# Sixteen loads issued by ScalarE instead of SyncE in a cluster-attention and softplus-FFN kernel

## The chip, the cores and the metric

The kernel runs on one core of a Trainium2 chip. Time is device time in microseconds (us) for one execution of the whole program. Its engines work from queues of their own, in order: TensorE (PE, with the weight loads PEld beside it), VectorE (DVE), ScalarE (ACT), GpSimd (POOL) and SyncE (SP), which computes nothing and issues DMAs.

## The reference, cut to what matters

Attention over 4 batches, 8 heads, 768 positions of 64 numbers, in which a query sees only the keys of its own cluster (16 centroids for each head); then a dense feed-forward with a softplus.

```
q_assign = argmax(einsum(q / |q|, c / |c|));  k_assign = the same of k
scores   = where(q_assign == k_assign, q k^T / 8, -1e9)
attn     = softmax(scores) @ v                       # (4, 8, 768, 64)
x        = attn as 3072 tokens of 512
out      = softplus(x @ w_in) @ w_out                # w_in 512 x 2048, w_out 2048 x 512
```

The weights come as 64-bit floating point, the rest as 32-bit.

## The kernel before, in words

Products are made in 16-bit halves (a high part and what it leaves over), so most data are cast to a high part and subtracted to a low part before a matmul uses them.

**Passes and tiles.** Eight passes `pi`: four batches, two halves of 384 queries each. A tile `t` is one head `n` and 128 queries; there are 24 tiles to a pass, 192 in all. Tiles 0 to 23 (pass 0) take the way of `upright`, where scores come out already turned. From tile 24 on, `scores(t)` is a chain of six steps: PE multiplies queries by keys into `s` (L1079), DVE takes the row maximum `negm` (L1095), ACT the exponential `p` (L1103), ACT or POOL the high part (`ph<t>`, L1112), POOL or DVE the low part (`p<t>`, L1113), and SP issues a transposing DMA `pt<-phl` (`flip`, L307, called in L1133). `attend(t)` then multiplies `pt` by the values into `mbank` (L1173 to L1175). Four pairs of heads make an `x`, which is transposed too (`xT`), and `ffn1` (L1244 to L1246, 16 blocks of 128 columns a pass), `softplus` (L1265, L1266, L1281) and `ffn2` (L1645 to L1647) follow, one pass behind attention.

**Preparation.** `prep_k`, `prep_q` and `prep_v` load keys, queries and values of two or four heads (384 KB each; 192 KB for the first halves), cast and subtract them, transpose them (from head 4 on by DMA: `kt<-kn`, `qt<-qn`, `qt<-n`) and find the clusters. `prep_weights(step)` loads one of 32 blocks of weights (512 KB, steps 0 to 15 of `w_in`, 16 to 31 of `w_out`) as raw 64-bit words into room that is later used by other data, and turns it into two 16-bit halves: ACT (L414), then `wb` (L372 or L374), DVE (L421), `wh` (L424), `w` (L425 to L429). The loads wait for room: a block for the block that had the same room before, keys, queries and values of later heads for one of two `raw` buffers.

**What sets the order.** Every piece of work is an operation of a generator. `either(key, first, second)` has two engines for it, and the key's presence in `SWAPPED` takes the second. The string `PLAN` names, two characters an operation, which generator goes next; there are 3543 of them, and since each engine runs its own instructions in order, `PLAN` is the order of every queue. The numbers in ns beside the operations (450 for a load) served when the string was made; nothing reads them when the kernel is built. `FILL` puts idle matmuls (L266) ahead of some of the first PE operations. Before the change all loads, stores and transposes are issued by SP, so they wait for each other in that one queue.

Of the kernel before, what the change touches and what calls it, by code (L numbers as in the profile page):

```python
# [37 lines left out]
SWAPPED = ('E1_0', 'S1l_1', 'S1l_3', 'S2_1', 'S2_3', 'S2h_0', 'S2l_0', 'S3l_0', 'S3l_2', 'S4_0', 'S4_2', 'S4_3', 'S4h_2', 'S4l_1', 'S4l_2', 'T1a_0', 'T1a_1', 'T1a_2', 'T1a_3', 'T1c_1', 'T1c_2', 'T1c_3', 'T1h_1', 'T1h_3', 'T1l_3', 'T2a_0', 'T2a_2', 'T2c_0', 'T2c_2', 'T2h_1', 'T2h_2', 'T2h_3', 'T2l_0', 'T2l_2', 'T2l_3', 'T3a_0', 'T3a_1', 'T3a_2', 'T3a_3', 'T3b_0', 'T3b_2', 'T3c_0', 'T3c_1', 'T3h_0', 'T3h_2', 'T3h_3', 'T3l_1', 'T3l_2', 'T3l_3', 'T4a_0', 'T4h_2', 'T4h_3', 'T4l_0', 'T4l_2', 'g0_2', 'g0_3', 'g0_6', 'g0_7', 'g1_1', 'g1_3', 'g2_0', 'g2_2', 'g3_1', 'g3_3', 'g3_4', 'g3_5', 'g3_7', 'g4_2', 'g4_4', 'g4_6', 'g5_5', 'g5_7', 'g6_1', 'g6_5', 'g7_1', 'g7_2', 'g7_4', 'g7_5', 'g7_6', 'g7_7', 'gh1_0', 'gh1_1', 'gh1_4', 'gh1_5', 'gh1_6', 'gh2_2', 'gh2_3', 'gh2_4', 'gh2_5', 'gh3_1', 'gh3_2', 'gh3_3', 'gh3_4', 'gh3_5', 'gh3_6', 'gh3_7', 'gh4_0', 'gh4_1', 'gh4_2', 'gh4_3', 'gh4_4', 'gh4_5', 'gh4_7', 'gh5_0', 'gh5_1', 'gh5_2', 'gh5_3', 'gh5_4', 'gh5_6', 'gh6_0', 'gh6_2', 'gh6_3', 'gh6_6', 'gh7_0', 'gh7_2', 'gh7_3', 'gh7_5', 'k0_0', 'k10', 'k16', 'k2', 'kT0_0_1', 'kT0_2_1', 'kT1_0_1', 'kT1_2_0', 'kT1_2_1', 'kh18', 'kh2', 'kh22', 'kh24', 'kh28', 'kh30', 'kh6', 'm12_2_0', 'm16_4_0', 'm4_0_0', 'mw_0', 'p103', 'p104', 'p108', 'p109', 'p111', 'p113', 'p115', 'p126', 'p138', 'p141', 'p142', 'p154', 'p157', 'p162', 'p165', 'p168', 'p174', 'p176', 'p182', 'p183', 'p187', 'p190', 'p191', 'p25', 'p27', 'p29', 'p30', 'p31', 'p33', 'p34', 'p35', 'p36', 'p37', 'p39', 'p40', 'p43', 'p44', 'p45', 'p58', 'p61', 'p63', 'p69', 'p76', 'p84', 'p85', 'p86', 'p87', 'p89', 'p95', 'p96', 'p98', 'ph100', 'ph102', 'ph103', 'ph104', 'ph106', 'ph107', 'ph108', 'ph109', 'ph110', 'ph111', 'ph112', 'ph115', 'ph116', 'ph117', 'ph119', 'ph120', 'ph121', 'ph122', 'ph123', 'ph124', 'ph125', 'ph126', 'ph127', 'ph128', 'ph129', 'ph130', 'ph131', 'ph133', 'ph135', 'ph136', 'ph137', 'ph140', 'ph141', 'ph142', 'ph143', 'ph145', 'ph146', 'ph147', 'ph149', 'ph150', 'ph151', 'ph152', 'ph153', 'ph154', 'ph156', 'ph157', 'ph158', 'ph159', 'ph160', 'ph163', 'ph164', 'ph165', 'ph167', 'ph168', 'ph169', 'ph170', 'ph171', 'ph173', 'ph174', 'ph175', 'ph176', 'ph177', 'ph178', 'ph181', 'ph184', 'ph185', 'ph189', 'ph190', 'ph24', 'ph28', 'ph36', 'ph42', 'ph48', 'ph50', 'ph51', 'ph52', 'ph53', 'ph56', 'ph59', 'ph60', 'ph63', 'ph65', 'ph66', 'ph68', 'ph71', 'ph75', 'ph76', 'ph78', 'ph80', 'ph81', 'ph82', 'ph83', 'ph86', 'ph87', 'ph88', 'ph89', 'ph90', 'ph91', 'ph94', 'ph95', 'ph97', 'ph98', 'ph99', 'q0_0_0', 'qT0_0', 'qT1_1', 'qh4_0', 'u1', 'u10', 'u2', 'u21', 'u22', 'u23', 'u27', 'u31', 'u33', 'u35', 'u9', 'v10', 'v2', 'v22', 'v28', 'v30', 'v8', 'vh0', 'vh12', 'vh14', 'vh16', 'vh18', 'vh20', 'vh22', 'vh24', 'vh26', 'vh28', 'vh30', 'vh8', 'w10', 'w11', 'w16', 'w18', 'w20', 'w21', 'w26', 'w31', 'w9', 'wb0', 'wb1', 'wb10', 'wb12', 'wb13', 'wb14', 'wb15', 'wb16', 'wb17', 'wb18', 'wb2', 'wb20', 'wb21', 'wb22', 'wb23', 'wb24', 'wb25', 'wb26', 'wb27', 'wb28', 'wb30', 'wb31', 'wb4', 'wb5', 'wb7', 'wb8', 'wb9', 'wh1', 'wh12', 'wh13', 'wh14', 'wh15', 'wh16', 'wh17', 'wh21', 'wh23', 'wh24', 'wh26', 'wh27', 'wh29', 'wh3', 'wh30', 'wh31', 'wh5', 'wh6', 'wh7', 'wh8', 'x1_3', 'x2_2', 'x3_0', 'x4_2', 'x5_2', 'x6_1', 'x7_1', 'x7_3', 'xh0_0', 'xh0_2', 'xh0_3', 'xh1_0', 'xh1_1', 'xh1_3', 'xh2_0', 'xh2_1', 'xh2_2', 'xh3_0', 'xh4_1', 'xh4_2', 'xh5_1', 'xh5_2', 'xh6_0', 'xh6_1', 'xh6_2', 'xh6_3', 'xh7_0', 'xh7_2', 'xh7_3', 'zk0', 'zk10', 'zk14', 'zk16', 'zk22', 'zk26', 'zk28', 'zk30', 'zk4', 'zk8', 'zq0_0_1', 'zq0_1', 'zq12_2', 'zq12_3', 'zq16_4', 'zq24_6', 'zq24_7', 'zq28_6', 'zq28_7', 'zq4_1', 'zq8_2', 'zq8_3')  # L38

REBASE = 2.0**-112  # L40
# [8 lines left out]
    "dodq081x1zdrcdcedrc821dy1u230acac7211z0723dw1wcb21210dcf2523dv1ycd2527c80d2327dpdr29ca0b20cd23290dcf2523dr1q"
    "2b2bcb2522cg22dz2d2bcg0cdx29250a1q2722e00d2d252d22272fcf2429cc2f2bc90dca0d0d2d27c9e2cgcbch26ce0dcf2h270d2h0d"  # L50
    "2928cdcicfchcg29e32b2jch0d0c2jci2b0d2a2fe4cg0dch2l0d2f2dci2h222dcj2cccck0dcje52n2lch2f2ncj2e2p2e2h222f2j2h0d"
    "0a2jck2e2pe72l2n2p0d2j2h2e1q2ncl2l2gcicc2l0c2p2i2j2nck22cj0d2lcecl2p0ecj2nci2eckcm2ece2pck2r2t0e2r2k0e2r2t2v"
    "2me80ccl2r2vcn2t2r2t2x2t2e2vcme92x2o2q2v2xclcm2v2z2q312xco2q0f2qcn2z310eeb0ecm2r2z31cocn2x0e2t312qec2s2vcl2u"
# [1670 lines left out]
```

## Time and profile before

| | |
|---|---|
| median of 3 runs | 804.58 us (803.59 to 806.15) |
| the profiled execution's own time | 803.36 us |
| its span, first to last instruction | 801.6 us |
| granted clock of TensorE | 1.00 throughout |
| PE busy | 782.3 us, 98% |
| PEld, DVE busy | 520.8 us (65%), 623.3 us (78%) |
| ACT, POOL busy | 450.4 us (56%), 632.1 us (79%) |
| DMA | 138.45 MB, 173 GB/s; 377 issues of SP in the plan, 259 of them transposes |

Busy time of an engine does not count the issuing of DMAs; an issue stands in the timeline of SP's queue (SPq), from its start until the queue goes on. "Idle before" is the time for which an engine stood still ahead of an instruction, and the arrow names what ended it. The chain of waits is followed back from the last instruction: at each step to what released it.

### The profile page before, as it was taken

How to read it: one execution, taken by the hardware profiler on the slowest of the kernel's cores; microseconds unless marked ns; L12 is line 12 of the kernel's file. 1: busy time of each engine (PE TensorE's matmuls, PEld its weight loads, DVE VectorE, ACT ScalarE, POOL GpSimd, SP SyncE). 2: the span in 40 equal slices, each digit the busy share in tenths (PEclk: the TensorE clock that was granted, in tenths of full speed). 3: DMA queues.
4: the chain of work that ended last, by engine and by line, in shares of the span. 5: the costliest groups of instructions: out<-in, count | busy, mean ns of one | idle time of the engine just before them, and what ended most of it. 6: DMA issues, size and time to landing. Idle time of an engine off the chain costs nothing.

```text
span 801.6 us, 19510 instructions
## 1 busy us (share of the span) xinstructions
PE 782.3 (98%) x7933; PEld 520.8 (65%) x7933; DVE 623.3 (78%) x977; ACT 450.4 (56%) x721; POOL 632.1 (79%) x521
## 2 busy tenths in 40 slices
PE   7999988999999999999999999999999999999998
PEld 6899655556566666556656666556656565676787
DVE  7998989878577869586787867676866768777796
ACT  6889979646656655355444455353554454625540
POOL 5787766758889879777589999888898898995463
DMA  8999999999999999999999999999998785730101
GB/s 271 257 239 240 204 235 234 244 224 178 195 195 197 188 189 169 225 193 196 154 156 210 187 187 184 181 176 210 170 157 172 127 160 90 141 61 1 47 2 60
DMA packets 411851, 138.45 MB, mean 173 GB/s; under 512 B 388464, under 2 KB 405360, under 8 KB 411760
## 3 DMA queue, kind: packets, MB, share of 16 engines
q1 hardware_dynamic: 411760, 137.19, 87.5%
q8 instruction: 62, 1.02, 0.5%
q14 instruction: 29, 0.24, 0.1%
HBM read 35.68 MB, written 6.29 MB: 52 GB/s over the span
## 4 chain that ended last, share of the span: by engine, by line
PE 79%; DMA 8%; ACT 4%; POOL 3%; DVE 2%; issue 1%; SPq 1%; POOLq 0%; DVEq 0%; ACTq 0%
PE s L1079 11%; PE h L1244 9%; PE h L1246 9%; PE h L1245 9%; PE o L1645 7%; PE o L1647 7%; PE o L1646 7%; PE mbank L1175 3%; PE mbank L1173 3%; PE mbank L1174 3%; DMA pt<-phl 3%; PE mbank L1169 3%; PE m L1523 2%; PE m L1522 2%; PE m L1524 2%
## 5 line engine op out<-in xcount | busy, mean ns | idle before, releaser
L1095 DVE TENSOR_REDUCE negm<-s 128x1 f32<-128x768 f32 x168 | 158.7, 951 | 79.3 <-PE s L1079 78.1
L1117 POOL TENSOR_TENSOR phl<-p,phl 128x768 f16<-128x768 f32 x117 | 204.3, 1752 | 7.2 <-ACT phl L285 4.3
L1103 ACT ACTIVATE p<-s,negm 128x768 f32<-128x768 f32 x168 | 150.0, 897 | 95.4 <-DVE negm L1095 72.5
L1244 PE MATMUL h<-xT,wi 128*128 128x384 f16 x512 | 166.7, 326 | 0.6 <-DVE fg L1281 0.6
L1246 PE MATMUL h<-xT,wi 128*128 128x384 f16 x512 | 166.9, 326 | 0.0
L1245 PE MATMUL h<-xT,wi 128*128 128x384 f16 x512 | 166.8, 326 | 0.0
L1265 ACT ACTIVATE fa<-h 128x384 f32<-128x384 f32 x128 | 62.5, 489 | 136.6 <-PE h L1246 136.4
L1079 PE MATMUL s<-kt,qt 128*128 128x384 f16 x672 | 134.4, 326 | 2.9 <-DMA qt<-n 1.8
L285 POOL CAST phl<-p 128x768 f16<-128x768 f32 x103 | 94.0, 917 | 46.9 <-ACT p L1103 23.9
L1173 PE MATMUL mbank<-vb,pt 128*128 128x65 f16 x1008 | 106.1, 192 | 6.2 <-DMA pt<-phl 6.1
L1647 PE MATMUL o<-wo,gh 128*128 128x512 f16 x288 | 109.1, 379 | 0.0
L1646 PE MATMUL o<-wo,gh 128*128 128x512 f16 x288 | 109.1, 379 | 0.0
L1645 PE MATMUL o<-wo,gh 128*128 128x512 f16 x288 | 109.1, 379 | 0.0
L1174 PE MATMUL mbank<-vb,pt 128*128 128x64 f16 x1008 | 106.1, 192 | 0.0
L1175 PE MATMUL mbank<-vb,pt 128*128 128x65 f16 x1008 | 105.7, 194 | 0.0
L1173 PEld LDWEIGHTS <-pt 128*128 128x128 f16 x1008 | 93.1, 98 | 18.8 <-DMA pt<-phl 9.1
L1174 PEld LDWEIGHTS <-pt 128*128 128x128 f16 x1008 | 92.8, 97 | 9.3
L1175 PEld LDWEIGHTS <-pt 128*128 128x128 f16 x1008 | 92.9, 97 | 0.0
L1079 PEld LDWEIGHTS <-qt 128*128 128x128 f16 x672 | 62.0, 98 | 44.4 <-DMA qt<-n 3.0
L1281 DVE SCALAR_TENSOR_TENSOR fg<-fa,h 128x384 f32<-128x384 f32 x104 | 56.2, 546 | 28.6 <-ACT fa L1266 24.2
L1246 PEld LDWEIGHTS <-wi 128*128 128x128 f16 x512 | 50.0, 98 | 33.2
L1244 PEld LDWEIGHTS <-wi 128*128 128x128 f16 x512 | 50.0, 98 | 31.8 <-issue 0.5
(309 smaller groups left out, 1645.0 us busy)
## 6 DMA issues: line engine op xcount, KB each, us to landing
wo<-in_moe_w_in_dram SPq DMA_DIRECT2D x16, 512.0 KB, 6.3
wo<-in_moe_w_out_dram SPq DMA_DIRECT2D x14, 512.0 KB, 4.8
rawk<-in_k_dram SPq DMA_DIRECT2D x15, 384.0 KB, 4.2
...
pt<-phl SPq DMA_TRANSPOSE x168, 4.2
...
```

The source lines that it names most:

```text
L1079: nc.tensor.matmul(st[:, j, :SH], qt[:, s, i], kt[:, s, NT // 2 * j : NT // 2 * (j + 1)], start=(s == 0), stop=(s == 1),)
L1095: yield op("DVE", 950, lambda: nc.vector.tensor_reduce(negm, st[:, :, :SH], AX.XY, ALU.max, negate=True))
L1117: lambda e: e.tensor_tensor(phl[:, u, 1], p32, phl[:, u, 0], ALU.subtract),
L1173: nc.tensor.matmul(av, pt[:, 0, c], vb[:, c, D : 2 * D + 1], start=(c == 0), stop=False)
L1174: nc.tensor.matmul(av[:, :D], pt[:, 0, c], vb[:, c, :D], start=False, stop=False)
L1175: nc.tensor.matmul(av, pt[:, 1, c], vb[:, c, D : 2 * D + 1], start=False, stop=(c == NT - 1))
L1244: nc.tensor.matmul(hp, w[0], x[0], start=(c == 0), stop=False)
L1245: nc.tensor.matmul(hp, w[0], x[1], start=False, stop=False)
L1246: nc.tensor.matmul(hp, w[1], x[0], start=False, stop=(c == NP - 1))
L1645: nc.tensor.matmul(po, g[0], wo[:, f, 0, 0], start=(f == f0), stop=False)
L1646: nc.tensor.matmul(po, g[0], wo[:, f, 0, 1], start=False, stop=False)
L1647: nc.tensor.matmul(po, g[1], wo[:, f, 0, 0], start=False, stop=(f == f0 + NF // 2 - 1))
```

## The change: what it does

Plain loads and stores get a key (`move`), so that ACT can be taken instead of SP. Sixteen keys are swapped; all else of that kind stays on SP, as do all transposes. `PLAN`, `SWAPPED` and `FILL` differ up to operation 1149 of 3543. From there on the order of every queue and the side of every operation are as before.

```diff
-FILL = {0: 26, 2: 3, 4: 8, 8: 3, 9: 3, 14: 19, 19: 9, 22: 4, 24: 4, 26: 3}
+FILL = {0: 26, 2: 3, 4: 11, 8: 4, 14: 15, 19: 8, 20: 3, 22: 4, 24: 3, 26: 3}
...
+    'lk1', 'lk12', 'lk14', 'lq12_2', 'lq8_3', 'lv10', 'lv12', 'lw13', 'lw22', 'lw23', 'lw25', 'lw26', 'lw29', 'lw30', 'lw5', 'lw6',
...
+ISSUE = 450
...
-    engines = {"DVE": nc.vector, "ACT": nc.scalar, "POOL": nc.gpsimd}
+    engines = {"DVE": nc.vector, "ACT": nc.scalar, "POOL": nc.gpsimd, "SP": nc.sync}
...
-    def load(dst, src, nbytes, ns=450):
-        return op("SP", ns, lambda: nc.sync.dma_start(dst, src), dma=nbytes / 290.0)
+    def move(key, dst, src, nbytes, ns=450, **opt):
+        return either(key, ("SP", ns), ("ACT", ISSUE), lambda e: e.dma_start(dst, src), dma=nbytes / 290.0, **opt)
...
-        yield load(raw64, src[:, c, e * WC : (e + 1) * WC], P * WC * 8)
+        yield move(f"lw{step}", raw64, src[:, c, e * WC : (e + 1) * WC], P * WC * 8)
...
-            yield load(kf, rows(k, n, 0, NT, 2), P * 2 * NT * D * 4)
+            yield move(f"lk{n}", kf, rows(k, n, 0, NT, 2), P * 2 * NT * D * 4)
```

The sixteen, with their place among the 3543 operations (read by following `PLAN` through `Order.run`) and the start of their issue by SP in the trace of before:

| load | place before, after | issued at, us |
|---|---|---|
| lk1 (head 1, second half of the first keys) | 6, 3 | 1.65 |
| lw5, lw6, lw13 | 175, 130; 200, 162; 329, 330 | 28.15; 28.84; 47.55 |
| lw22, lw23 | 569, 521; 592, 540 | 92.08; 96.45 |
| lw25, lw26 | 666, 669; 709, 691 | 114.42; 123.20 |
| lk12 | 807, 773 | 143.93 |
| lw29, lw30 | 852, 837; 880, 853 | 149.72; 152.63 |
| lk14, lv10 | 893, 883; 928, 887 | 156.27; 166.93 |
| lq12_2, lv12 | 947, 964; 989, 1001 | 169.28; 177.68 |
| lq8_3 | 1123, 1100 | 209.97 |

Other sides changed in the same stretch: 18 operations from DVE to POOL and 13 back, 23 from ACT to POOL and 19 back, 10 from DVE to ACT and 4 back. Of those between operations 500 and 870, ACT gives POOL the high parts `ph29`, `ph32`, `ph45`, `gh0_0`, `gh0_2`, `gh0_3`, `kh12`, and `wb21`, `wh25`, `wh28`; it takes from POOL `ph28`, `ph42`, `vh8`, `xh1_0`, `wb19`, `wb29`, `wh21`, `wh23`, `wh26`. `p25` goes from DVE to POOL, behind `p24`; `kh2`, at the start, from POOL to ACT, ahead of the second copy of the first turned keys.

In SP's queue some neighbours change places: the first queries' load stands third instead of fourth; the values of heads 8 and 9 (`lv8`) are loaded behind the transpose of tile 31 instead of ahead of it; tile 54 is transposed ahead of tile 55 instead of behind it.

## Rows read from the trace of the kernel before

**Rows 1.** Windows: busy us (instructions) of PE, PEld, DVE, ACT, POOL; clock; DMA share; GB/s

```profile
0.00:40.00 40.00, 34.64 (x496) 30.36 (x496) 34.28 (x105) 29.49 (x52) 25.99 (x40) 1.00 0.87 264
...
80.00:150.00 70.00, 63.94 (x670) 41.84 (x669) 63.12 (x100) 63.15 (x103) 49.47 (x38) 1.00 1.12 225
150.00:215.00 65.00, 61.66 (x594) 36.58 (x593) 48.24 (x84) 34.70 (x55) 49.27 (x41) 1.00 1.06 208
```

**Rows 2.** Waits of PE, 80 to 215 us: us in total, times, longest

```profile
PE mbank L1173 <- DMA pt<-phl: 5.5, 6, 1.7
```

**Rows 3.** Timeline of PE: start, us, instruction [idle before <-releaser]

```profile
88.86 0.20 PE L1173 MATMUL mbank<-vb,pt 128*128 128x65 f16 x1 [0.62 <-DMA pt<-phl]
...
115.07 0.20 PE L1173 MATMUL mbank<-vb,pt 128*128 128x65 f16 x1 [1.02 <-DMA pt<-phl]
...
139.31 0.20 PE L1173 MATMUL mbank<-vb,pt 128*128 128x65 f16 x1 [1.65 <-DMA pt<-phl]
...
159.41 0.42 PE L588 MATMUL sim_k<-cents,kt 128*128 128x32 f16 x10 [0.79 <-DMA kt<-kn]
...
179.84 0.34 PE L1079 MATMUL s<-kt,qt 128*128 128x384 f16 x1 [1.22 <-DMA qt<-n]
...
209.77 0.20 PE L1173 MATMUL mbank<-vb,pt 128*128 128x65 f16 x1 [1.33 <-DMA pt<-phl]
```

**Rows 4.** Chain of waits, parts of 0 to 215 us: start, us, what

```profile
2.13 4.37 DMA rawq<-in_q_dram
...
105.81 2.38 SPq L307
...
108.24 4.01 DMA rawv<-in_v_dram
...
143.93 3.55 DMA rawk<-in_k_dram
...
163.05 5.10 DMA wraw<-in_moe_w_out_dram
```

**Rows 5.** Timeline of SP's queue: start, us, issue

```profile
1.65 0.43 SPq L302 DMA_DIRECT2D rawk<-in_k_dram  x1
...
92.08 1.00 SPq L302 DMA_DIRECT2D wo<-in_moe_w_out_dram  x1
...
108.92 1.65 SPq L307 DMA_TRANSPOSE pt<-phl  x1
...
204.09 2.91 SPq L307 DMA_TRANSPOSE pt<-phl  x1
...
209.97 0.50 SPq L302 DMA_DIRECT2D rawq<-in_q_dram  x1
```

**Rows 6.** Transposes of tiles, 80 to 215 us: ns min/median/max, first and last start; landing

```profile
L307 SPq DMA_TRANSPOSE pt<-phl x34: 1273/1630/4162, 82.8 to 214.8; - x34
...
DMA to landing us min/median/max: 3.7/4.7/6.8
```

**Rows 7.** Timeline of DVE and POOL: the low parts of tiles 24, 25, 31, 54

```profile
80.78 1.97 POOL L1117 TENSOR_TENSOR phl<-p,phl 128x768 f16<-128x768 f32 x1
...
82.44 1.12 DVE L1117 TENSOR_TENSOR phl<-p,phl 128x768 f16<-128x768 f32 x1 [0.33 <-ACT phl L285]
...
102.91 1.25 DVE L1117 TENSOR_TENSOR phl<-p,phl 128x768 f16<-128x768 f32 x1
...
199.33 3.25 POOL L1117 TENSOR_TENSOR phl<-p,phl 128x768 f16<-128x768 f32 x2 [0.34 <-ACT phl L285]
```

**Rows 8.** Waits of ACT, 80 to 150 us

```profile
ACT wo L414 <- DMA wo<-in_moe_w_out_dram: 5.0, 3, 1.9
```

**Rows 9.** Lines of ACT, 80 to 150 us: busy us, mean ns | idle before

```profile
L285 ACT CAST phl<-p 128x768 f16<-128x768 f32 x17 | 14.0, 830 | 1.1 <-DMA pt<-phl 1.0
...
L372 ACT ACTIVATE wo<-wo 128x512 int32<-128x512 uint8 x10 | 6.7, 670 | 0.0
...
L285 ACT CAST wo<-wo 128x512 f16<-128x512 f32 x6 | 3.9, 648 | 0.0
```

More of the change, by code (lines that the diff above doesn't have):

```diff
@@ L49 @@
[L49 to L53, printed above, removed]
@@ new lines @@
+    "1hd4071f0bd908d409c6c71h1j1fd41h1f1j0b1h1ld4c81f1lc6dg091n1l1jc31j1f0b1h1g1n1hdic51p1jc5c7081p081n1j1rc4081i"
+    "c9090b1r1t1vc808c31p08dj081r1k091t1lc30508c41n08091p1x1v0bdl1x1lca1tdl1l1xc9c50b1v1z0bcb1v091nc41z1n0b051m08"
+    "1r0909c6091tc71x09c6cc0b0907211p071pdn09dk211odo1r0bdoca1qcddo0bc8dqc71t1r1tdscb1qc61zc91v1q1q21ca1x1sdu1vdo"
+    "dsdp1zdpdvccc81x1zc9c7cb1udmc923dxc81wcd1z2321ce21dpdy2521251q1ycbdp0ddtca27252329cecfcd2720230d0b292b0ddw25"
+    "232b2222220dcgdz2d2b1qchcfe12d230aca2927252207cf07272d2f24ce252fcc29ci270dcg0c26cbe22b2h0dcdce27cf0d22ch0d2f"
@@ new lines @@
+    "cg0d2he30d0d29cc0c28292b0d2f2jcf2bcgcgchchcd0dcjci2j222d0d2a2le42d2c2d2l0dck0cci2h2n2f2e2hci2n1qcc2e2pcj222f"
+    "ck2e2j2p2ee62lcj2je7ch2h2n0d2p2l2jck2hci0d2n2g2p2l2i2jcl0a2ncl2l2eckcj2p0e0de82n2pcm0ecl2r2t2r2rcm0ecl2kcj2t"
+    "2e2v2v2tcnck2m0c2x2o2v2t2vce2rco2r2q2te9cl2x2v2x2z2e31cm2q0e2q0e2qcm2zcp2x0f310e2z2r2q2t3331cm2s2q2z2x0e2vcn"
+    "cqeb0e2qcocz0e31352u33cp2w2xec330e2z0fcz0f37ee31cocz35eeee0ecocz350e370eefczco2z330e0fcn0e39330eefcz37352yeg"
+    "efed393b31eg35cp0eczegcncz3930ehcr3beh3937cn0feh3b3dcqef320f0icr37320f3dcz0fei32ef33cz32czejcz0f0e39ekd00icr"
@@ new lines @@
+    "eh0iel0f3f34cpekeleh3dd0ekcr35el32crcqcz3fcscz3b3fem3d36em0h0f3h3b370a3h393jczemcp380fctcq3f3hcseo3jen0i3hen"
+    "3d3fcqcz3lepcs3a3j3bep3hcz3d3lcsepczel3neq3l0i3ccs0h3jeq3lcuct3p0i3n3fel320g0i3e3e3jd00ieq0icz3pczcu3h3nczcz"
+    "etes3l3e0i0h3e3r3pepescu3t0ieuescu0kepeu3r3nczer3l3gcz3r3icu3p3j3teuctctev3nct0f3k3pcv3t3r3vev3t3m3vcv3rd00g"
+    "eu3xevczewczev3vcz3ney3x3t0k3p0kescvcz3z3rcv3xeyexcv3ocw3v0ies3z41ezeyd03t0kd0ez3eez41cx3qezcz3x3zf03vczf1d0"
+    "0i0g3x3q3vcwf0f2evd03xf1cw3ecz41f1czf30ncw0kd00jcwezf43q0kd00k0k3q0g3scxf5cx0kf4cxcyd0f43ud032f40kcx0n0k0kf7"
@@ L480, in prep_v @@
         for u in range(0, 2, 2 // parts):
-            yield load(
-                vf[:, u : u + 2 // parts], rows(v, n + u, 0, NT, 2 // parts), P * 2 * NT * D * 4 // parts, 450 * parts
+            yield move(
+                f"lv{n + u}", vf[:, u : u + 2 // parts], rows(v, n + u, 0, NT, 2 // parts), P * 2 * NT * D * 4 // parts, 450 * parts
             )
@@ L560, in first_half, with fill @@
         od.set(hk)
-    def fill(dst, src):
+    def fill(key, dst, src):
         src = src.unsqueeze(1).to_broadcast([1, dst.shape[1] * 4, 32])
         to = dst.rearrange("p c (a t) -> p (c a) t", t=32)
-        return op("SP", 450, lambda: nc.sync.dma_start(to, src), dma=60, tail=2000)
+        return move(key, to, src, 17000, tail=2000)
     TWIN = 10
@@ L697, in load_half @@
     def load_half(n, u, kf):
-        yield load(kf[:, u : u + 1], rows(k, n + u, 0, NT, 1), P * NT * D * 4)
+        yield move(f"lk{n + u}", kf[:, u : u + 1], rows(k, n + u, 0, NT, 1), P * NT * D * 4)
         od.set(("ld", n, u))
@@ L713, in lift @@
     def lift(n, kt0):
-        yield fill(kt0[EXTRA:ROWS], full[:1])
+        yield fill(f"fk{n}", kt0[EXTRA:ROWS], full[:1])
         od.set(("up", n))
@@ L754, in prep_q @@
         if n or pi:
-            yield load(qf, rows(q, n, passes[pi][1], QT, 4), P * c12 * D * 4)
+            yield move(f"lq{sfx}", qf, rows(q, n, passes[pi][1], QT, 4), P * c12 * D * 4)
         raw = qf
@@ L870, in first_q @@
         x = raw.rearrange("p h c d -> p (h c) d")[:, part]
-        yield load(raw[:, 2 * u : 2 * u + 2], rows(q, 2 * u, 0, QT, 2), P * n6 * D * 4)
+        yield move(f"lq0_0_{u}", raw[:, 2 * u : 2 * u + 2], rows(q, 2 * u, 0, QT, 2), P * n6 * D * 4)
         lo, hi = n1[:, part, :D], n1[:, part, D:]
@@ L1578, in send @@
         to = out_v[b, :, c0 : c0 + 2, e * HE : (e + 1) * HE] if w == 0 else out_v[b, :, c0 + 2 : c0 + 3, e * HE : (e + 1) * HE]
-        return op("SP", 60, lambda: nc.sync.dma_start(to, acc), dma=(128e3 if w else 256e3) / 290)
+        return move(f"so{b}_{row}_{e}_{w}", to, acc, 128e3 if w else 256e3, 60)
     def accs3():
@@ L1670, in store @@
         od.set(ok)
-        yield op("SP", 60, lambda: nc.sync.dma_start(out_v[b, :, c0 + i], acc), dma=256e3 / 290)
+        yield move(f"so{pi}_{i}", out_v[b, :, c0 + i], acc, 256e3, 60)
         od.set(ak)
```

30 lines of the change are left out of this document (10 added, 20 removed).

## The prediction

> **What bounds the kernel now.** I read the table of windows first. TensorE is busy nearly without a break from 215 us on; what it loses, it loses before that: 5.36 us of the first 40, 6.06 of the stretch 80 to 150 and 3.34 of 150 to 215 (length less PE's busy time) [rows 1]. The granted clock is 1.00 in every stretch, 2.4 GHz, so it is no part of the question. Since the order of every queue is untouched from operation 1149 on, which falls near 215 us (operation 1123 is the load issued at 209.97 [rows 5]), the change can only move the point at which that common remainder starts. The time at stake is therefore some 15 us of idle PE, 1.8% of the whole.
>
> Second, the waits of PE. Between 80 and 215 us the largest entry is the transposed tile: 5.5 us in 6 waits [rows 2]. The single gaps in PE's timeline show the rest: one wait each for a transposed key block (0.79) and a query block (1.22), beside those for `pt` [rows 3]. So a transpose that SP issues is what PE stands still for.
>
> Third, whether SP issued them late or the data were late. Tile 31's low part is done at 102.91 + 1.25 = 104.16 [rows 7], but its transpose is issued only at 108.92 [rows 5]: 4.8 us in the queue, and the gap of 1.02 at 115.07 is its landing [rows 3]. Tile 54 is done at 199.33 + 1.65 = 200.98, the first half of a pair on POOL [rows 7], and is issued at 204.09 [rows 5]: 3.1 us in the queue, with a gap of 1.33 behind it [rows 3]. Against that, tile 25 is done at 82.44 + 1.12 = 83.56 [rows 7]; with a median landing of 4.7 [rows 6] that is 88.3, and PE has it at 88.86 [rows 3], so that gap is due to the engines. So a part of the waits is SP's and a part isn't.
>
> Last, the chain of waits, which tells who else stands in that queue: it runs through SP's issue of a transpose at 105.81 into the load of values at 108.24, and later through the loads of keys at 143.93 and of weights at 163.05 [rows 4]. A load that is issued late by SP is itself on the path, not only in the way.
>
> **The change part by part.** All sums are against the profiled execution, 803.36 us (span 801.6 and 1.8 around it); the median of the runs shown is 1.22 higher.
>
> *The issues taken from SP.* The sixteen issues occupied SP's queue for 11.6 us in all, 0.72 on average; the first took 0.43 and the last 0.50, and one in the busy stretch 1.00 [rows 5]. SP is only relieved where it is behind; where it has caught up, the freed time is worth nothing. I go through the gaps:
> - 115.07: ahead of tile 31's transpose the issue at 92.08 (1.00) is gone, and the values' load that started at 108.24 [rows 4], 0.68 before the transpose [rows 5], now follows it. Together 1.68, more than the gap of 1.02: gain 1.02 (bounds 0 and 1.02).
> - 139.31: tile 38. The two loads that leave SP before it (lw25, lw26) were issued at 114.42 and 123.20 (the table of the sixteen), more than 16 us ahead of that landing, so SP may have caught up in between. Half the gap of 1.65: 0.83 (bounds 0 and 1.65).
> - 159.41: the keys of heads 12 and 13. Their load was issued at 143.93 and is on the chain [rows 4]; now it stands 34 operations earlier, which is near 137 (an estimate from the same table, between operation 709 at 123.20 and 807 at 143.93). The gap goes: 0.79 (bounds 0 and 0.79).
> - 179.84: queries, whose chain goes back to the weights' load at 163.05 [rows 4]. That load stays on SP, but four loads ahead of it leave (lk12, lw29, lw30, lk14: about 4 x 0.72 = 2.9). The rest of that chain is DVE and POOL work. Half: 0.61 (bounds 0 and 1.22).
> - 209.77: tile 54 now goes ahead of tile 55 and can be issued about 3 us earlier: 1.33 (bounds 0 and 1.33). This is the order, not the engine.
>
> Sum 4.6, at most 6.0. The gap at 88.86 stays, and I count none of the small ones.
>
> *The start.* The first queries' load, 2.13 to 6.50 on the chain [rows 4], has one issue of 0.43 [rows 5] less ahead of it. On the other side ACT gets the cast `kh2`, 0.83 by the same shape later [rows 9], ahead of a copy that the cluster search needs. Between -0.43 and +0.40; I take a gain of 0.3, nearer the row that is on the chain. `FILL` goes from 82 idle matmuls to 80, nothing.
>
> *The issues put on ACT.* No row shows an ACT issue. From the rows of SP it costs between 0.43 [rows 5] and, if it is held as a slow transpose is, 4.16 [rows 6]; I take the 0.72 that the same sixteen cost, as the nearest row to the same DMA. It matters where ACT is tight: 63.15 of 70 us in 80 to 150 [rows 1]. Six fall there (lw22, lw23, lw25, lw26, lk12, lw29): 4.3 us. The same stretch gives POOL six casts of 0.83, `kh12` alike, one `wb` of 0.67 and two `wh` of 0.65 = 7.8, and takes three casts of 0.83, a half one (0.42, an estimate from that), two `wb` and three `wh` = 6.2 [rows 9]: 1.6 less. Net 2.7 more on an engine with 6.85 us to spare, 5.0 of which it spends waiting for weights that land late [rows 8]. Earlier weights pay for a part of it. I take 1.0 on the path (bounds 0 and 2.7). What is queued behind each issue on ACT is the exponential or the cast of the next tile, and DVE, POOL and SP wait for these. After 150 ACT is busy 34.70 of 65 [rows 1]; an issue there is hidden behind its idle time, and costs its own 0.72 only where the cover is gone.
>
> *The other sides.* POOL takes nine operations more, about 5 subtractions of 1.65 [rows 7] and 4 casts, some 12 us by estimate. It was busy 124.7 us in the three stretches of 175 (25.99, 49.47 and 49.27 [rows 1]), so its total is covered; a single link that gets longer is not. `p25` moves behind `p24`, which ends at 82.75, and would end at 84.4 instead of 83.56 [rows 7]. Its tile has a gap of 0.62 already [rows 3]: a loss of 0.8 (bounds 0 and 1.3).
>
> *Sum.* -0.3 - 4.6 + 1.0 + 0.8 = -3.1: 800.3 for the profiled execution, 801.5 as a median.
>
> **The rivals.**
>
> *A. The DMA engines, not the queue, are the bound.* Their share in 80 to 150 is 1.12 [rows 1], and a tile lands 3.7 to 6.8 us after its issue, median 4.7, where the shortest issue took 1.27 and the longest 4.16 [rows 6]. If those long issues are the queue waiting for full rings, an earlier issue only lands later by as much. For: the share over 1. Against: the share is 1.06 from 150 to 215, where PE loses 5.1% in place of 8.7% [rows 1]. Then only the start and the order of tile 54 gain: -0.3 - 1.3 + 1.0 + 0.8 = +0.2, 804.8. The Trainium skill, "DMA: Bandwidth & Descriptors", section "Issuing engines are not separate DMA queues", says that DMAs of all engines run on the same 16 engines and that several issuers save issue time alone; by that rule this rival holds wherever issue time is not what is short.
>
> *B. Slower: the issue holds ACT.* SP is issuing transposes for most of 80 to 150, each for 1.63 in the median [rows 6]. If an issue on ACT must wait until SP's is through, six cost 0.72 + 1.63 = 2.35 each, 14.1 us, less the 1.6 that ACT gives away: 12.5 against 6.85 of idle time, so 5.7 lands on the path, and the tiles' gains are lost. -0.3 - 1.3 + 0.8 + 5.7 = +4.9: 809.5. It decides from (6.85 + 1.6) / 6 = 1.41 us for one issue on ACT, where the spare time is used up. For: issues of one kind of load already vary from 0.43 to 1.00 [rows 5]. Against: nothing in this trace has a second issuer. The Trainium skill, "Perfetto Trace Analysis", section "DMA Instruction - HWDGE (DVE, Sync)", says that the two sequencers share a descriptor generator, which is locked for one at a time, so that the other's issue includes a lock wait. No row here shows it; by that rule this rival's mechanism is there, and its size is open.
>
> *C. More than forecast.* Weights and keys that arrive early take away ACT's 5.0 us of waiting [rows 8] and all of PE's idle time past 80 us (6.06 + 3.34 [rows 1]): 804.58 - 0.3 - 9.4 = 794.9. Against: ACT works 90% of 80 to 150 [rows 1].
>
> **How the numbers follow.** A measurement of this kernel tells about 0.3% (2.4 us) from no change. Chances: forecast 0.42, A 0.24, B 0.22, C 0.12. The forecast's own range is 798.5 to 804.5: 0.30 of its 0.42 is faster than 802.2, 0.10 the same, 0.02 slower. A gives 0.02, 0.17 and 0.05; B 0, 0.03 and 0.19; C 0.12 faster. Together 0.44 faster, 0.30 the same, 0.26 slower. The range runs from 796.5, short of C, to 808.5, short of B's full price; about 0.17 lies outside.
>
> **What would show it.** Right: the rows of ACT's queue issue their loads in under 0.9 us; the gaps at tiles 31 and 54 and at the keys of head 12 are gone; ACT's wait for weights in 80 to 150 falls well below 5.0; and the part behind the common point takes as long as before. Rival A: tiles are issued earlier and land no earlier. Rival B: an issue on ACT above 1.4 us, and PE waits for ACT in place of SP. The forecast falls if PE's idle time before 215 us is not 2 to 5 us smaller.

## The result: slower by 0.55%, and the profile after

The changed kernel takes 810.04 us (median of 13 executions, 805.34 to 812.88), the kernel before 804.65 us on the same chip (13, 802.39 to 807.66). The ratio is 1.0055, interval 1.0038 to 1.0072: slower by about 4.4 us, where 801.5 was forecast. A second measurement gave 810.6 against 804.66, ratio 1.0062 (1.0041 to 1.0082).

The profiled execution of the changed kernel took 805.34 us, the fastest of its thirteen. So the trace shows a mild case; its span is 803.3 us, 1.7 longer than before, and a second profile (806.53 us) is read beside it below.

What stands against [rows 2] now, the waits of TensorE between 80 and 215 us (total, times, longest):

```profile
PE s L1080 <- ACT p L1104: 3.2, 1, 3.2
PE sim_k L589 <- DVE fg L1282: 2.7, 1, 2.7
PE mbank L1174 <- DMA pt<-phl: 1.7, 2, 1.5
```

The 5.5 us of waiting for transposes in six waits became 1.7 in two. In their place stand two long waits for ScalarE and VectorE, 3.2 and 2.7 us. The longest gap before was 1.65 [rows 3]. The windows of the changed kernel (columns as in [rows 1]) show what followed behind these two:

```profile
80.00:150.00 70.00, 63.46 (x647) 42.75 (x646) 66.76 (x98) 58.41 (x96) 48.44 (x36) 0.95 1.12 223
88.00:92.00 4.00, 0.77 (x18) 0.58 (x16) 3.86 (x7) 2.38 (x4) 2.12 (x3) 1.00 0.93 149
92.00:94.00 2.00, 2.00 (x25) 1.40 (x25) 1.97 (x5) 0.75 (x1) 0.00 (x0) 0.71 1.12 370
94.00:96.00 2.00, 2.00 (x8) 0.99 (x7) 1.97 (x5) 1.55 (x3) 1.42 (x2) 0.50 1.51 287
96.00:98.00 2.00, 2.00 (x43) 1.57 (x42) 1.79 (x2) 2.00 (x4) 1.92 (x2) 0.94 0.83 174
128.00:130.00 2.00, 0.05 (x1) 0.00 (x0) 2.00 (x3) 0.00 (x0) 1.42 (x2) 1.00 1.38 184
130.00:132.00 2.00, 1.24 (x31) 1.24 (x31) 2.00 (x5) 1.72 (x3) 1.92 (x2) 0.60 0.74 183
132.00:134.00 2.00, 2.00 (x25) 1.32 (x22) 1.50 (x3) 2.00 (x4) 2.00 (x2) 0.55 1.15 270
```

Read PE's busy time and the clock together. TensorE works 0.77 us of the four from 88 to 92 and nothing of the two from 128 to 130; right behind each, at full load again, its granted clock is 0.50 to 0.71, which is the lower level, 1.2 GHz, for most of some four microseconds. One minus the clock times the length of the windows, over the whole span, is 3.4 us; before it was 0.0. The idle time ahead of TensorE's instructions, added over the whole trace, fell from 16.15 to 14.10 us, 2.05 less. With the 3.4 of the clock that makes +1.35, where the spans differ by 1.7. The two agree, but not because these two terms are the loss. That shows when both traces are split where the last `u` product of pass 0 ends, at 76.78 us before and 78.51 after (windows of the kernel before, then of the changed one):

```profile
0.00:76.78 76.78, 71.42 (x923) 65.03 (x924) 67.47 (x159) 61.47 (x107) 55.56 (x70) 1.00 0.97 252
76.78:801.57 724.79, 710.85 (x7011) 455.76 (x7009) 555.83 (x818) 388.92 (x615) 576.58 (x452) 1.00 0.87 164
```

```profile
0.00:78.51 78.51, 73.50 (x921) 67.42 (x922) 64.80 (x148) 63.06 (x114) 62.14 (x75) 1.00 0.96 244
78.51:803.30 724.79, 712.55 (x7011) 457.92 (x7009) 556.92 (x819) 386.02 (x610) 579.68 (x456) 0.99 0.88 165
```

Behind that point both kernels take 724.79 us. TensorE stands still for 1.70 us less there and is busy for 1.70 longer, half of the 3.4 that the clock gives. The whole loss of this execution, 1.73 us, is already there when pass 0 ends, ahead of both long gaps. In pass 0 TensorE stands still for 0.35 us less, but is busy for 2.08 longer with the same products (two idle matmuls fewer). A part of that is its speed in the first 11 us: six products of the keys took 0.51 us at 9.79 before, and 0.80 at 9.89 after:

```profile
9.79 0.51 PE L536 MATMUL kT<-eye,kn 128*128 128x128 f16 x6
```

```profile
9.89 0.80 PE L537 MATMUL kT<-eye,kn 128*128 128x128 f16 x6
10.85 0.52 PE L537 MATMUL kT<-eye,kn 128*128 128x128 f16 x6
```

The profile lists no granted clock for these first microseconds and prints 1.00, so a lower clock is read here from the durations alone. The kernel before starts slowly too: the first 26 idle matmuls take 2.76 us in both, 0.106 each, where later ones take 0.056. In the second profile of the change the same products are as fast as before (0.51 at 9.96), and yet pass 0 ends 1.52 us late, now by idle time (6.79 us against 5.36). So the new start is late in both, for different reasons.

**The first gap.** All engines of the changed kernel from 85 us on (start, us, engine, line, instruction, idle before it):

```profile
85.24 3.28 POOL L1118 TENSOR_TENSOR phl<-p,phl 128x768 f16<-128x768 f32 x2 [0.98 <-ACT phl L286]
...
86.92 2.14 DVE L422 SCALAR_TENSOR_TENSOR wo<-wo 128x512 int32<-128x512 int32 x1 [0.65 <-POOL phl L1118]
...
89.11 0.33 ACTq L303 DMA_DIRECT2D wo<-in_moe_w_out_dram  x1
...
89.95 1.81 DVE L1096 TENSOR_REDUCE negm<-s 128x1 f32<-128x768 f32 x2
...
90.99 1.76 ACT L1104 ACTIVATE p<-s,negm 128x768 f32<-128x768 f32 x2 [0.51 <-DVE negm L1096]
...
91.94 0.65 PE L1080 MATMUL s<-kt,qt 128*128 128x384 f16 x3 [3.23 <-ACT p L1104]
```

The scores of t30 (91.94) wait for a PSUM slot, which the exp of t28 frees (90.99), which waits for the negated maximum of t28 on VectorE (89.95). Its scores were ready at 87.72, but VectorE was in a step of the weights' rounding from 86.92 to 89.06: 2.14 us instead of about 0.7. Three short operations (0.9 us in all) stood between that step and the maximum. Beside the step GpSimd ran the subtractions of t25 (`p25`, on VectorE before) and t26, until 88.52; VectorE's step ended 0.55 us after that, so some 1.5 us of it was waiting. By its row VectorE had also stood idle for 0.65 us ahead of the step, until a subtraction on GpSimd ended. Together that is 2.1 of the gap of 3.23. The Trainium skill, "SBUF — State Buffer", section "SBUF: two separate sides", says that VectorE, in an instruction with two inputs in SBUF, and GpSimd share one pair of ports under an exclusive lock, and that the one that comes second is blocked for the other's whole instruction. The rows agree: 2.14 us instead of 0.68, ended 0.55 us after GpSimd's.

**The second gap** (VectorE and GpSimd, then TensorE):

```profile
124.56 2.38 DVE L1118 TENSOR_TENSOR phl<-p,phl 128x768 f16<-128x768 f32 x1 [0.89 <-POOL phl L286]
126.87 1.65 DVE L422 SCALAR_TENSOR_TENSOR wo<-wo 128x512 int32<-128x512 int32 x1
...
130.17 0.54 DVE L1282 SCALAR_TENSOR_TENSOR fg<-fa,h 128x384 f32<-128x384 f32 x1
```

```profile
124.49 1.64 POOL L1118 TENSOR_TENSOR phl<-p,phl 128x768 f16<-128x768 f32 x1
126.09 1.87 POOL L430 TENSOR_TENSOR wo<-wo 128x512 f16<-128x512 f32 x1
```

```profile
130.76 0.43 PE L589 MATMUL sim_k<-cents,kt 128*128 128x32 f16 x10 [2.71 <-DVE fg L1282]
```

The same pattern: `fg` of f7, which frees the slot for the product of the keys n10, stands on VectorE behind a subtraction of 2.38 us (0.95 when alone) and a weight step of 1.65 (0.7), each ending 0.6 to 0.8 us after GpSimd's; another subtraction (0.95) and a maximum (0.94) stand between them and `fg`. `p35` at 124.49 ran on VectorE before.

**The issues.** ScalarE's queue holds the loads for far less than assumed, and SP's transposes became no shorter in the median (compare [rows 6]; ns min/median/max, first and last start):

```profile
L303 ACTq DMA_DIRECT2D wo<-in_moe_w_out_dram x5: 334/335/343, 89.1 to 152.8; - x5
```

```profile
L308 SPq DMA_TRANSPOSE pt<-phl x34: 1429/1810/3204, 84.6 to 214.9; - x34
...
DMA to landing us min/median/max: 3.7/5.2/7.5
```

All sixteen take 0.33 to 0.50 us. ScalarE's wait for weights in 80 to 150 fell from 5.0 us [rows 8] to:

```profile
ACT wo L415 <- DMA wo<-in_moe_w_out_dram: 0.5, 1, 0.5
```

### The profile page after: what moved, and what is told of

Read it like the earlier page. It is cut to its first block, busy times and chain, and to the rows that moved or that the text cites. A ratio compares the mean times of both kernels' runs of the same rounds, so it can differ in the third digit from the quotient of the medians.

```text
span 803.3 us, 19525 instructions
## 1 busy us (share of the span) xinstructions
PE 786.1 (98%) x7931; PEld 525.3 (65%) x7931; DVE 621.7 (77%) x966; ACT 449.1 (56%) x723; POOL 641.8 (80%) x530
## 4 chain that ended last, share of the span: by engine, by line
PE 82%; DMA 6%; DVE 5%; ACT 3%; issue 2%; POOL 1%; ACTq 0%; SPq 0%; DVEq 0%; POOLq 0%
PE s L1080 12%; PE h L1245 9%; PE h L1247 9%; PE h L1246 9%; PE o L1646 7%; PE o L1648 7%; PE o L1647 7%; DMA pt<-phl 5%; PE mbank L1176 3%; PE mbank L1174 3%; PE mbank L1175 3%; PE mbank L1170 2%; PE m L1525 2%; PE m L1523 2%; PE m L1524 2%
## 5 line engine op out<-in xcount | busy, mean ns | idle before, releaser
L1118 POOL TENSOR_TENSOR phl<-p,phl 128x768 f16<-128x768 f32 x120 | 207.4, 1735 | 9.2 <-ACT phl L286 6.3
```

The lines of the kernel that those rows point to most:

```text
L1118: lambda e: e.tensor_tensor(phl[:, u, 1], p32, phl[:, u, 0], ALU.subtract),
```

## The experiments

"Gaps" is the idle time ahead of TensorE's instructions in the profile, less that of the kernel before (16.15); "clock" is one minus the granted clock, summed over the span in steps of 2 us; "fills" are added idle matmuls at 0.056 us (44 took 2.47). The last column is what the span really gained on 801.6. Medians and ratios are against the kernel before on the same chip (804.1 to 805.6).

| kernel | us | ratio (95%) | gaps | clock | fills | sum | span |
|---|---|---|---|---|---|---|---|
| the change | 810.04 | 1.0055 (1.0038 to 1.0072) | -2.1 | 3.4 | | 1.3 | 1.7 |
| the change again | 810.6 | 1.0062 (1.0041 to 1.0082) | 2.4 | 1.7 | | 4.1 | 2.8 |
| old order, loads on ScalarE | 815.22 | 1.0120 (1.0098 to 1.0142) | 2.4 | 10.3 | | 12.7 | 12.6 |
| new order, loads on SyncE | 822.49 | 1.0209 (1.0193 to 1.0226) | 10.8 | 8.5 | | 19.3 | 18.5 |
| new start, old rest | 808.25 | 1.0030 (1.0016 to 1.0043) | 1.8 | 3.4 | | 5.2 | 6.1 |
| old start, new rest | 809.32 | 1.0047 (1.0025 to 1.0070) | 1.2 | 3.4 | | 4.6 | 4.7 |
| old order, five loads | 805.9 | 1.0016 (1.0003 to 1.0029) | 1.4 | 0 | | 1.4 | 2.6 |
| old order, eleven loads | 813.37 | 1.0116 (1.0092 to 1.0140) | 4.8 | 5.1 | | 9.9 | 9.6 |
| change, two fills | 807.95 | 1.0047 (1.0031 to 1.0064) | -1.9 | 0 | 4.5 | 2.6 | 3.4 |
| change, smaller fills | 809.56 | 1.0059 (1.0043 to 1.0075) | 1.2 | 1.7 | 3.1 | 6.0 | 6.2 |
| change, second fill | 810.04 | 1.0047 (1.0028 to 1.0067) | 4.9 | 3.4 | 2.5 | 10.8 | 9.4 |
| loads on ScalarE, three fills | 810.52 | 1.0076 (1.0058 to 1.0094) | -0.2 | 3.4 | 5.4 | 8.6 | 9.0 |
| before, three fills | 804.67 | 1.0005 (0.9992 to 1.0018) | -1.7 | 0 | 2.1 | 0.4 | 3.1 |
| change, seven places moved | 809.08 | 1.0058 (1.0033 to 1.0083) | 4.2 | 5.1 | | 9.3 | 10.2 |
| moved, and five fills | 807.74 | 1.0043 (1.0030 to 1.0056) | -4.4 | 0 | 7.2 | 2.8 | 2.6 |
| change, two sides back | 815.2 | 1.0127 (1.0087 to 1.0167) | 4.3 | 12.0 | | 16.3 | 11.0 |

The sum meets the span within 1.5 us in fourteen of sixteen; it is 5.3 too high in the last row, 2.7 too low for the kernel before with fills. That doesn't show that its terms are the causes: the clock column leaves out the slow start of each execution and counts a fall in full, and in the first row the two errors cancel (2.08 us of slower work in pass 0 left out, 1.70 of 3.4 counted too much). A profile is one execution: the same kernel gave gaps of -2.1 and +2.4.

**Taking the change apart.** The old order, sides and start, with the sixteen loads on ScalarE at their old places:

```diff
 # PLAN and FILL of the kernel before
-SWAPPED = (...)
+SWAPPED = (..., 'lk1', 'lk12', 'lk14', 'lq12_2', 'lq8_3', 'lv10', 'lv12', 'lw13', ...)
```

> Order and sides of before; only the sixteen loads are issued by ACT, at their old places in the order. Theory 'order' (the new order and sides cost the time, the issuer does not): an ACT issue takes 0.33 to 0.50 us as in the trace of the change, 16 of them about 6 us on ACT, and SP gets 11.6 us back, so 800 to 805 us, same or a little faster than before. Rival 'loads' (the second issuer costs the time, by loads that push between transposes or by holding ACT): 807 to 811 us, most of the loss of 5.4 us.

The complement, PLAN and sides of the change with the sixteen names out of SWAPPED:

> New order, sides and idle matmuls; the sixteen loads go back to SP at their new places. Theory 'order': still slow, 809 to 814 us, since the order is kept and SP is loaded with 11.6 us more. Rival 'loads': back near before, 803 to 807 us.

And the two halves of the order, cut after operation 472, each with its own sides and loads:

> The first 472 operations (up to about 78 us) in the new order with the new sides, four of the sixteen loads on ACT among them; then the old order and sides. Theory 'order, start': the change is 1.8 us late when the first pass ends at 78 us, and that lasts: 806 to 808 us. Theory 'order, middle' (two long idle stretches of TensorE at 92 and 131 us, each with a fall of its clock): 803.5 to 805.5 us, like before.

> The first 472 operations in the old order, the rest in the new one, with twelve loads on ACT. Theory 'order, start': 802 to 805 us. Theory 'order, middle': idle stretches of 2 us and more with a fall of the granted clock in 85 to 140 us, 807 to 811 us. If the parts add, the two hybrids lose 5.4 us together.

The halves cost 2.7 and 3.8 us (808.25, just above the range of 'order, start', and 809.32, in that of 'order, middle'). Together that is about what the whole costs, so no single place makes the loss. The loads alone cost 9.7 us, the order and sides alone 16.9, more than any range given for them, and both together 5.4: the parts don't add, each is dear without the other. A reason can be read from where a load's issue falls. SP issued the load of weight step 30 at 152.63 before (its timeline):

```profile
152.63 0.84 SPq L302 DMA_DIRECT2D wraw<-in_moe_w_out_dram  x1
```

On ScalarE, at the same place of the same order, it comes at 166.18, when that kernel is some 9 us behind, so some 4.7 us later than the old order had it (ScalarE, VectorE and TensorE of the old order with loads on ScalarE):

```profile
166.18 0.33 ACTq L303 DMA_DIRECT2D wraw<-in_moe_w_out_dram  x1
170.79 0.67 ACT L415 ACTIVATE wo<-wraw 128x512 f32<-128x512 f32 x1 [4.17 <-DMA wraw<-in_moe_w_out_dram]
...
171.37 0.65 ACT L373 ACTIVATE wraw<-wraw 128x512 int32<-128x512 uint8 x1
```

```profile
172.05 0.69 DVE L422 SCALAR_TENSOR_TENSOR wraw<-wo,wraw 128x512 int32<-128x512 int32 x1 [3.96 <-DMA qt<-qn]
...
177.08 0.36 DVE L623 TENSOR_TENSOR eq_k<-eq_k,best_k 128x192 f16<-128x192 f16 x1
```

```profile
177.49 0.34 PE L730 MATMUL cnt<-eq_k,ones 128*128 128x192 f16 x1 [3.04 <-DVE eq_k L623]
```

SP had run ahead of the arithmetic. ScalarE comes to the load only when the work in front of it is done, and its next instruction is the first that needs the data: it stands still for 4.17 us, VectorE behind it for 3.96 (the row names a transpose of queries, but the step reads what ScalarE's second one, L373, wrote, and starts as that ends, at 172.02), and the marks `eq_k` of the keys n12, next in VectorE's order, reach TensorE late. Behind the gap of 3.04 the clock is low (windows of the same kernel, and those of an earlier fall, behind a gap of only 0.69 us at 59.17):

```profile
178.00:182.00 4.00, 4.00 (x52) 2.73 (x50) 3.93 (x6) 2.25 (x4) 3.28 (x2) 0.50 1.16 219
```

```profile
60.00:62.00 2.00, 1.98 (x17) 1.97 (x17) 1.97 (x5) 1.96 (x6) 1.83 (x2) 0.61 1.09 344
62.00:70.00 8.00, 8.00 (x50) 7.48 (x50) 4.42 (x9) 3.06 (x5) 4.04 (x4) 0.50 0.65 157
```

In the new order on SP it is the other way round. Two loads that ScalarE issues at 160.75 and 161.18 in the changed kernel come 14 us later when SP has them. That kernel is 7 us behind there (the exp ahead of them starts at 166.52 instead of 159.37); the other 7 they stand in SP's queue, behind transposes and loads that wait for room (ScalarE's queue in the changed kernel, then SP's in the new order with loads on SP):

```profile
160.75 0.39 ACTq L303 DMA_DIRECT2D rawk<-in_k_dram  x1
...
161.18 0.50 ACTq L303 DMA_DIRECT2D rawv<-in_v_dram  x1
```

```profile
170.04 4.72 SPq L308 DMA_TRANSPOSE pt<-phl  x2
174.80 0.85 SPq L303 DMA_DIRECT2D rawk<-in_k_dram  x1
175.76 0.42 SPq L303 DMA_DIRECT2D rawv<-in_v_dram  x1
```

In these rows each order has its loads where its issuer needs them. Which loads are dear on ScalarE was asked by a split of the sixteen, in the old order:

> The kernel before with only the five loads on ScalarE that stand where it has room: the second half of the keys of block 0 at the start, and V n10, the queries n12, V n12 and the queries n8 of the last pair, all after 160 us, where ScalarE is busy 34.7 of 65 us. Theory 'ScalarE in order' (in the old order a load on ScalarE stands behind unfinished exps and weight steps and comes late, or holds them; it costs where ScalarE is full): within 1.5 us of the kernel before, 803.5 to 806 us. Theory 'each load costs' (any load on ScalarE costs its issue and more): 5/16 of the 9.7 us that all sixteen cost in the old order, 3 us: 807 to 808.5 us.

> The complement: the kernel before with the other eleven loads on ScalarE (nine of weights from 28 to 153 us, keys n12 and n14), where ScalarE is busy nine tenths of the time. Theory 'ScalarE in order': nearly all of the 9.7 us, 812 to 817 us. Theory 'each load costs': 11/16 of it, 810.5 to 812 us. In its profile the difference of the spans should come out as the difference of TensorE's gaps plus what the clock lost, within 1.5 us, as it does in the ten profiles so far.

Five at the start and after 160 us cost 1.7 us, eleven between 28 and 157 us cost 9.2. The theory of a price for each load (3 and 6.7) is out, and ScalarE in order, where it is full, fits both. But nine of the eleven are loads of weights, and none of the five is; whether that or the full ScalarE makes them dear is not shown. Neither group gained anything in the old order.

**The clock.** Idle matmuls ahead of a gap keep TensorE at work and bring nothing earlier that it waits for.

> The changed kernel once more, for a second profile and a ratio on the same chip as the three beside it. Theory 'clock' (what the change costs is mostly the granted clock, which falls to half behind stretches in which TensorE stood still for about 3 us, and only the smaller part is the standing still itself): in this profile too every stretch of clock 0.5 to 0.6 lies right behind a long gap of TensorE, two to four of them, and one minus the clock of the run, times the span, is 3 to 6 us. Theory 'gaps' (the gaps alone make the time): the clock is 0.997 or more and the gaps of TensorE between 75 and 215 us add up to 10 us or more, where the kernel before has 7.3. Both: a median of 808 to 812 us.

This second profile has the gaps of 3.23 at 91.72 and 2.83 at 130.48 again, with a fall behind the second alone (1.7 us). By itself it meets what 'gaps' said and not what 'clock' said: a clock of 0.997, and 11.7 us of standing still between 75 and 215 us, where the kernel before has 9.7 counted the same way. Over all executions one minus the granted clock is 5.2 and 4.6 us of the change's span in the two measurements, and 0.5 to 1.6 of the kernel before's.

```diff
-FILL = {..., 24: 3, 26: 3}
+FILL = {..., 24: 3, 26: 3, 128: 44, 171: 36}
```

> The changed kernel with idle matmuls in its two long gaps: 44 ahead of the scores of tile t30 and 36 ahead of the key block n10 (a matmul onto spare columns of mbank, which the kernel has already at its start). TensorE waits as long as before for the exp and for fg, but has work meanwhile: some 2.2 and 1.8 us at 0.05 us each. Theory 'clock': the two falls behind these gaps (1.7 us each in the profile of the change) go, 2 to 4 us of 810 us: 806 to 808 us, clock 0.997 to 1. Theory 'gaps': no gain, 809 to 812 us, since nothing that TensorE waits for comes earlier.

> The old order with the sixteen loads on ScalarE at their old places (815.2 us) and idle matmuls in the three gaps of its profile behind which the clock falls: 12 ahead of the queries' product of n0 (gap 0.69 us at 59, then half the clock for 11 us), 34 ahead of the attention of t38 (1.98 us at 145), 50 ahead of the count of n12 (3.04 us at 177). Theory 'clock': of the 9.2 us that its profile loses to the granted clock most comes back: 806 to 809 us. Theory 'gaps': the loads on ScalarE delay what TensorE waits for, and fills don't bring it earlier: 814 to 817 us.

In the old order with loads on ScalarE the fills gain, from 815.2 to 810.5 (ratios 1.0120 and 1.0076, the intervals just apart), about half of the loss and less than the 806 to 809 of 'clock'; the clock's share over all executions went from 6.0 to 1.9 us. In the change no fall is left in the profile and the clock's share is 0.9, but the median came down by only 2.7 us, into the range of 'clock', and the intervals overlap. The timeline of TensorE with the two fills shows a cost of the means:

```profile
91.07 2.47 PE L267 MATMUL mbank<-ones,eye 128*128 128x120 f16 x44 [1.37 <-DVE x L1199]
93.38 0.81 PE L1080 MATMUL s<-kt,qt 128*128 128x384 f16 x4
```

The fills write into `mbank`, so they had to wait for VectorE to read it, and then held the scores of t30 until 93.38, 1.4 us later than in the profile without them. About 0.5 of that is theirs: the exp of t28 starts 0.98 later in this execution as it is (91.97 instead of 90.99). With 12 there (`128: 12, 171: 44`), and with none (`171: 44`):

> The changed kernel with 12 idle matmuls ahead of the scores of t30 (0.6 us; 44 held them up by 1.4 us) and 44 ahead of the key block n10. Theory 'clock' (3.6 us of the loss): clock 0.997 or more and 805.5 to 807 us. Theory 'half' (the clock is worth what the two larger fills brought, 2.7 us, and the rest is order): 807.5 to 808.5 us. If 12 are too few to keep the clock, the fall behind the first gap is in the profile and the time 808 to 809.5 us.

> The changed kernel with idle matmuls at the second place alone, 44 ahead of the key block n10. Theory 'clock': one of the two falls goes, 1.7 us or a little more, 808 to 809 us, granted clock 0.996 in the mean. Theory 'gaps': no gain, 810 to 811 us.

Neither gained anything that can be told from the change, though the clock's share is 2.8 and 2.7 us instead of 4.6 to 5.2, and no fall is left behind the second gap (with 12 and 44 there is one at 172.6 us instead, with 44 alone one at 8 us and the one behind the first gap). So a microsecond of low clock in this kernel isn't a microsecond of time; why not, whether because TensorE would have waited at full clock too, is not shown. The kernel before has nothing to win there:

> The kernel before, loads on SyncE, with idle matmuls ahead of three of its own gaps (10 ahead of the attention of t31, 16 of t38, 12 of t54), to see what the clock still costs the kernel before: its executions have a granted clock of 0.9985 in the mean, 1.2 us of its span. Theory 'clock': clock 0.999 to 1, 803.5 to 805 us, at most 1.2 us faster, which this measurement can hardly tell from no change. Against it: fills in front of an attention that is not late hold it up by 0.5 to 0.8 us each, up to 2 us slower.

**The order of VectorE.** Seven moves in the changed PLAN: the negated maximum of t28 ahead of weight step 19 on VectorE, its exp ahead of that step's cast on ScalarE; the two last operations of softplus f7 and the negated maximum of t39 ahead of weight step 25, with what this takes along on ScalarE.

> The changed kernel with seven places of its order moved and nothing else: on VectorE the negated maximum of t28 stands ahead of the weight step w19, and fg of f7 and the negated maximum of t39 ahead of the weight step w25; on ScalarE the exp of t28 ahead of the step of w19, and softplus f7 ahead of the exp of t38. Theory 'order' (both long gaps come from short steps on the way to TensorE that stand behind a weight step which takes 1.6 to 2.2 us when GpSimd works beside it): the gap of 3.2 us goes to about 1, that of 2.7 to under 1, with them both falls of the clock; 5 us or more of the two places, 804 to 807 us if nothing else comes late. Theory 'loads' (the loads on ScalarE are what makes the change slow): within 1 us of the change, 809 to 811 us.

Both gaps shrink: VectorE's step takes 0.68 us now that GpSimd is through, and t30 waits 1.05.

```profile
88.73 0.96 DVE L1096 TENSOR_REDUCE negm<-s 128x1 f32<-128x768 f32 x1 [1.48 <-PE s L1080]
89.61 0.68 DVE L422 SCALAR_TENSOR_TENSOR wo<-wo 128x512 int32<-128x512 int32 x1
```

```profile
90.74 0.48 PE L1080 MATMUL s<-kt,qt 128*128 128x384 f16 x2 [1.05 <-ACT p L1104]
...
178.75 0.45 PE L589 MATMUL sim_q<-cents,qt 128*128 128x32 f16 x10 [3.25 <-DMA qt<-qn]
```

The gap at the keys n10 is gone. But other gaps are new in this profile: 1.60 and 1.51 us at 96.12 and 98.84, with the clock low behind them, 2.33 at 147.45, and the last row, 3.25 at 178.75, in and behind which the clock is low again. The time is the same as the change's, and not the 804 to 807 us of 'order'. Shrinking the two gaps did not win the time back. Fills at five places where this kernel stood still took the clock's share to 0.4 us, and the time by no more than the intervals (1.0058 to 1.0043):

> The changed kernel with the seven places moved as in the second of the order experiments, and idle matmuls ahead of the five places at which the profile of that one stood still for more than 0.9 us (14 ahead of the scores of t30, 22 and 32 ahead of the attentions of t26 and t38, 15 ahead of the feed-forward f4, 45 ahead of the queries' product of n8). Theory 'clock and order': the falls of the clock go (0.998 to 1) and the gap of 3.2 us stays shortened: 804 to 807 us, at best level with the kernel before. If gaps only move on to other places: 808 to 810 us.

Last, the sides: `p25` and `p35` back on VectorE, two names out of some hundred.

> The changed kernel with the subtractions of tiles t25 and t35 back on VectorE, as in the kernel before; order and loads as changed. Theory 'sides' (GpSimd's subtraction beside VectorE's weight step is what makes the negated maximum of t28 and fg of f7 late): the weight step w19 takes about 0.7 us instead of 2.15, that gap of 3.2 us shrinks to 2 or less and its fall of the clock goes or shortens: 806.5 to 808.5 us. Theory 'order' (the steps stand in front whoever works beside them; VectorE gets 0.95 us more work for each of the two): the gaps stay at 2.5 us or more, 809.5 to 812 us.

The second gap fell from 2.71 to 0.60, the first from 3.23 to 2.40: at 86.24 another step on VectorE now takes 2.14 us beside t26 on GpSimd. And the kernel is 11 us slower than before, outside what either theory said, with new gaps of 1.8 to 2.8 us at 143 and from 173 to 180, and the clock low in most of 88 to 98 and 174 to 186:

```profile
88.00:98.00 10.00, 7.14 (x75) 4.57 (x75) 9.70 (x17) 8.25 (x12) 5.31 (x5) 0.66 1.09 247
...
174.00:186.00 12.00, 7.39 (x65) 4.24 (x65) 6.40 (x14) 4.55 (x8) 4.60 (x4) 0.57 1.02 204
```

## Why the prediction was wrong

- *The gaps of [rows 3]* (-4.6 forecast): the number came, the reason didn't; this step failed. The five waits are gone, 6.0 us of them. But the tiles were not there earlier, TensorE came later. Tile 31 has its low part at 106.15, waits 5.85 us in SP's queue instead of 4.76, and lands at 115.9 instead of 115.0; TensorE comes to it at 119.29 instead of 115.07 (the changed kernel):

```profile
105.21 0.94 DVE L1118 TENSOR_TENSOR phl<-p,phl 128x768 f16<-128x768 f32 x1
...
112.00 2.47 SPq L308 DMA_TRANSPOSE pt<-phl  x1
...
119.29 0.19 PE L1174 MATMUL mbank<-vb,pt 128*128 128x65 f16 x1
```

  Tile 38 is issued 3.3 us later than before (136.37) and tile 54 2.9 later (206.99), and TensorE comes to them 4.3 and 6.8 later. Of the three only tile 54 lost its time in SP's queue (0.1 us instead of 3.1), by the new order as forecast; tile 38 lost a third of its own (1.6 instead of 2.5). The sum took the waits off the time as if TensorE kept its old times. They went because it was late, and two new waits of 5.9 us stand in the same stretch.
- *The issues on ScalarE* (+1.0): the size was off. 0.72 each was assumed, 0.33 to 0.50 measured, so the six between 80 and 150 cost about 2.1 instead of 4.3 us; ScalarE was 58.41 us busy there instead of 63.15 [rows 1]. Rival B, an issue that waits for SP's transposes and decides from 1.41 us, fell in its mechanism though it had the sign. By the rule of the Trainium skill, "Perfetto Trace Analysis", cited with it, the lock would have to show in ScalarE's rows; the longest of sixteen is 0.50.
- *Rival A* (an earlier issue lands no earlier): not tested, since the tiles were not issued earlier. One lands 5.2 us after its issue in the median instead of 4.7 [rows 6].
- *The other sides* (+0.8): this step failed. `p25` was priced by its own tile alone: on GpSimd it would be done 0.8 us later. What it did to the order of the engine it left was not priced. Beside GpSimd's 3.28 us of subtractions a step of VectorE took 2.14 us instead of 0.68, and behind that step stood the maximum that t30's slot hung on; the same happened at 124.56 with `p35`. The two waits of TensorE behind them are 5.9 us. With both back on VectorE they are 3.0, so about half of them goes with the two sides. What that is worth in time is open: that kernel is slower, not faster.
- *The granted clock* was called "no part of the question", since it was 1.00 before, and so stood at nothing. It was 1.00 beside gaps of up to 1.65 us; behind two of about 3 us it fell. Over all executions the clock's share rose from 0.5 to 1.6 us to 4.6 to 5.2, and covering two falls brought 2.7 us of median, not told from none by the intervals. So some of the loss is the clock, how much is open.
- *The start* (-0.3): wrong sign. The new start alone makes the kernel 2.7 us slower (1.0016 to 1.0043). In the two profiles of the change pass 0 ends 1.7 and 1.5 us later, which is the whole loss of the first and half that of the second. The last `u` product starts at 76.5 to 77.9 us in the four profiles with the old start and its loads of weights on SP, and at 77.9 to 80.0 in the nine with the new start and its loads on ScalarE.
- The condition for failing was met: TensorE's idle time before 215 us is 0.95 us smaller (14.10 against 15.05), not 2 to 5. All the signs of being right came true beside it: issues of under 0.9 us, the gaps gone, 0.5 us of waiting for weights, and the part behind the common point as long as before (ScalarE's exps run 1.9 us later than before at 233 us and 1.7 at the end). None of them says whether TensorE comes to a place earlier.

What stays open is how the 4.4 to 5.4 us divide. The two long gaps could be shortened, and the falls covered, one by one and together, without the kernel getting back to the time of before; the best of these tries stayed 0.43% above it. Each repair has other waits in its profile, and which ones differs from one execution to the next. What makes the new start slower was not tried at all.
